# Two softmax attentions on one core: the matmuls of a step as tiles of 64 rows by 32 columns

## The chip, the cores and the metric

The kernel runs on one core of a Trainium2 chip. The core has five engines that run side by side, each with its own order of instructions: TensorE multiplies matrices (PE in the profile, PEld for its loading of weights), VectorE (DVE) and ScalarE (ACT) work element by element and can read the results of TensorE, GpSimd (POOL) works element by element on the large on-chip memory (SBUF) alone, and SyncE (SP) issues most of the transfers (DMA). TensorE writes its results to PSUM, a memory of eight banks, each of 128 partitions by 512 numbers of four bytes. A matmul multiplies a matrix of weights, loaded before, with data that stream through the array, one column after the other. The array of 128 rows by 128 columns can be used as several smaller tiles, and the profile shows several of them at work at the same time.

The metric is the device time of one execution in microseconds (us).

## What is computed

Two attentions over the same 2048 positions of 576 features are mixed by a gate. B has 32 heads with one shared key and value (unit 0 to 31 in the kernel), A has 32 heads with keys and values of their own (units 32 to 63). Each head is 18 wide.

```python
qkv = (x @ wqkv).reshape(B, S, 3, H, Dh)          # A; H = 32, Dh = 18
scores = einsum("bhqd,bhkd->bhqk", q, k) * Dh ** -0.5
p = softmax(scores, axis=-1)
o = einsum("bhqk,bhkd->bhqd", p, v)
a = o.transpose(0, 2, 1, 3).reshape(B, S, D) @ wo
# b is the same with q = x @ wq per head, one k = x @ wk and one v = x @ wv for all heads
g = sigmoid((x * gate_w).sum(-1, keepdims=True))
return g * a + (1 - g) * b                        # S = 2048, D = 576, f32
```

## The kernel before

**Stages.** First `project` (L205) and `project_v` (L249) compute queries, keys and values from x and the weights, as three products of a high and a low part, on the whole array. Then come 1024 steps, 16 for each of the 64 units. Step i of unit u works on keys 128 i to 128 i + 127 for scores and on queries 128 i to 128 i + 127 for maxima. The projection of the output (`out_proj`, L545) is cut into pieces, called units of work in the schedule, which are put between the steps; a tail adds the last head (`last_out`, L602).

**What a step does.** Queries and keys are split in two halves of 16 bits, so a product is one matmul over 54 rows (three products of 18 rows each), to which 2 rows with the maximum are added for the scores. The same rows lie twice in SBUF, from partition 0 (`SB`) and from partition 64 (`MB`).

- `step_scores` (L440; matmul L446): 128 keys by 512 queries, over partitions 0 to 55, into a bank of the pool `ps_s` (three banks). ScalarE takes the exponential of it (L453) into a tile `pt` in SBUF. Four of these make a step.
- `step_max` (L397; matmul L409): 128 queries by 512 keys, over partitions 64 to 117, into a bank of the pool `ps_m` (four banks). VectorE reduces it to a maximum per query (L418). These run 22 steps ahead (`LEAD`), since the maxima go into the scores. Every second step, one of its four maxima is replaced by the product `x` with the difference of two blocks of keys; ScalarE takes its Relu (L412), and a fused VectorE instruction (L415) adds it to another block and takes the maximum. So a pair of steps has eight score matmuls, eight of maxima (one of them `x`), nine instructions on ScalarE and seven on VectorE.
- `step_pv` (L455; matmul L459): the product of values (19 columns, one of them ones, for the sum) with `pt`, over 128 keys, in f32, for each of the four blocks of 512 queries. Block j goes to partitions 32 j to 32 j + 18 of one accumulator `acc` (one bank), so the four matmuls use four tiles of 128 rows by 32 columns. It adds up over the 16 steps.
- After step 15, `head_out` (L467) copies `acc` to SBUF on VectorE (L469), and SP's queue carries the parts to the rows of the head and to `sum_d`. The first value product of the next unit waits for the copy.

**Order.** The order of work on TensorE, and with it that on ScalarE and VectorE, is written out by hand. The loop at L695 goes through pairs of steps (T, T + 1) and through the words of a string: `sA0` is score block 0 of the first step of the pair, `mB2` maximum block 2 of the second step (of the unit 22 steps later), `x` the difference product, `p` and `f` the first and second half (256 columns each) of the value product of step T - 2, `P` both halves in one; `h` and `H` the two halves for step T - 1, `Q` both in one; `U` a unit of the output's projection, 12 matmuls over the whole array that take a bank of `ps_m`. `PLAIN` is the usual string, `UNIT` that of a pair with units, `END` that of a pair with T a multiple of 16, after which a head is copied out, `AFTER` that of the pair behind it, `ALONE` that of the last 11 pairs, when no maxima are left. `LEADS` and `FIRST` belong to the pairs before and at T = 0.

## Time and profile before

| | us |
|---|---|
| median of two runs | 2734.95 (2734.13 to 2735.77) |
| the profiled execution, its own time | 2735.79 |
| its span in the trace | 2734.0 |

The granted clock of TensorE was 0.991 of full speed in the mean. The first score of the steps starts at about 315 us and the last at about 2701 us of the span.

A page of the profile has the busy time of each engine, the span in slices, the DMA queues, the chain of work that ended last (followed back from the last instruction, at each step to what released it), and groups of instructions by line: `L453 ACT ACTIVATE pt<-ps ... x4052 | 2093.1, 637` says that line 453 ran 4052 times on ScalarE, was busy for 2093.1 us in all and 637 ns in the mean for one. Instructions of one engine overlap, so the mean of one is longer than its share of the time. The start-to-start distance in rows of the timeline (start in us, duration in us, engine, line, operation, output from input, count) is the better measure of what one costs. Some records of matmuls are missing from the trace, a few per cent.

### The profile page before, as it was taken

The numbers are of one execution on the slowest core, as the hardware profiler recorded it, in microseconds if no ns is written. First come the engines' busy times: TensorE is split into PE (matmuls) and PEld (weight loads), VectorE is DVE, ScalarE is ACT, GpSimd is POOL, SyncE is SP. The second block draws the span as 40 slices with busy tenths as digits, with TensorE's granted clock in tenths as the row PEclk, the third lists the DMA queues.
The fourth block names the chain that finished last, engine by engine and source line by source line (L and its number), as shares of the span: only waits on it lengthen the run. The fifth ranks groups of instructions, "written<-read, shape, count | busy, mean of one in ns | idle before, by whom it ended". The sixth has DMA issues, their size and how long they took to land.

```text
span 2734.0 us, 57725 instructions
## 1 busy us (share of the span) xinstructions
PE 2663.3 (97%) x22160; PEld 958.8 (35%) x22160; DVE 2430.7 (89%) x4582; ACT 2384.1 (87%) x4768; POOL 231.0 (8%) x438
## 2 busy tenths in 40 slices
PE   5899999999999999999999999999999999999999
PEld 3688522222222222222222333333333332223444
DVE  5345899999999999999999999999999999998875
ACT  3232499999999999999999999999999999998875
POOL 2221000001000200110110001000100020001000
PEclk9899999999999999999999999999999999999998
DMA  7232100001100100110132112112221122122312
GB/s 197 76 118 90 51 20 20 20 18 53 35 17 23 54 27 20 45 43 20 30 66 85 40 51 84 54 40 57 72 66 47 44 61 64 39 64 88 89 36 94
DMA packets 135321, 151.49 MB, mean 55 GB/s; under 512 B 55709, under 2 KB 104765, under 8 KB 133846
## 3 DMA queue, kind: packets, MB, share of 16 engines
q1 hardware_dynamic: 116156, 123.59, 16.2%
q10 hardware_dynamic: 14120, 13.65, 1.5%
q0 software_dynamic: 4768, 10.56, 1.2%
q8 instruction: 174, 2.85, 0.5%
q14 instruction: 103, 0.84, 0.1%
HBM read 92.02 MB, written 46.45 MB: 51 GB/s over the span
## 4 chain that ended last, share of the span: by engine, by line
ACT 54%; PE 37%; DVE 6%; DMA 2%; SPq 1%; issue 1%; DVEq 0%; ACTq 0%
ACT pt L453 48%; PE acc L459 12%; PE ps L446 11%; ACT xb L412 6%; PE ps L210 6%; PE pm L575 4%; DVE mx L418 3%; PE ps L252 2%; PE pm L409 2%; SPq L56 1%; DVE oe L469 1%; DVE junk L415 1%; DMA xs<-xT 0%; DVE oacc L629 0%; DVE oacc L583 0%
## 5 line engine op out<-in xcount | busy, mean ns | idle before, releaser
L453 ACT ACTIVATE pt<-ps 128x512 f32<-128x512 f32 x4052 | 2093.1, 637 | 68.4 <-PE pm L409 60.2
L418 DVE TENSOR_REDUCE mx<-pm 128x1 f32<-128x512 f32 x3096 | 1940.2, 682 | 89.5 <-PE pm L409 74.6
L446 PE MATMUL ps<-qs,ksb 56*128 56x512 f16 x2688 | 818.4, 380 | 10.8
L409 PE MATMUL pm<-ksb,qs 54*128 54x512 f16 x2364 | 738.5, 383 | 2.6 <-DVE mx L418 1.6
L459 PE MATMUL acc<-pt,vb 128*19 128x512 f32 (+1 forms) x6136 | 592.3, 458 | 1.9
L459 PE MATMUL acc<-pt,vg 128*19 128x256 f32 (+1 forms) x5664 | 579.5, 481 | 2.3 <-DVE oe L469 0.5
L409 PEld LDWEIGHTS <-qs 54*128 54x128 f16 x4096 | 330.0, 93 | 248.1 <-issue 195.2
L446 PE MATMUL ps<-qs,ksa 56*128 56x512 f16 x1364 | 404.4, 379 | 4.8 <-ACT pt L453 1.3
L446 PEld LDWEIGHTS <-ksb 56*128 56x128 f16 x2688 | 175.0, 94 | 622.5 <-issue 573.9
L409 PE MATMUL pm<-ksa,qs 54*128 54x512 f16 x1232 | 384.8, 382 | 0.6 <-ACT xb L412 0.4
L415 DVE CUSTOM_DVE_ANT_0 junk<-pm,xb 128x512 bf16<-128x512 f32 x500 | 339.9, 680 | 0.0
L412 ACT ACTIVATE xb<-pm 128x512 f32<-128x512 f32 x500 | 316.5, 633 | 0.0
L446 PEld LDWEIGHTS <-ksa 56*128 56x128 f16 x1408 | 89.3, 94 | 328.9 <-issue 299.0
L459 PEld LDWEIGHTS acc<-pt,vb 128*19 128x19 f32 x6136 | 104.1, 96 | 223.7 <-issue 206.6
L459 PEld LDWEIGHTS acc<-pt,vg 128*19 128x19 f32 x5664 | 96.0, 97 | 222.9 <-issue 204.9
L428 POOL TENSOR_SCALAR mt<-mt 128x32 f32<-128x32 f32 x64 | 18.6, 290 | 1616.4 <-DVE mt L426 1616.4
L214 ACT ACTIVATE ph<-ps,tv 128x512 f16<-128x512 f32 x56 | 38.5, 687 | 122.0 <-PE ps L210 114.5
L409 PE MATMUL pm<-kdb,qs 54*128 54x512 f16 x372 | 141.5, 380 | 0.0
L220 DVE SCALAR_TENSOR_TENSOR pl<-ps,tv,ph 128x512 f16<-128x512 f32 x56 | 42.0, 751 | 93.8 <-ACT ph L214 75.4
L210 PE MATMUL ps<-xh,wh 128*128 128x512 f32 x280 | 76.4, 403 | 3.3 <-DVE xh L277 2.6
L210 PE MATMUL ps<-xh,wl 128*128 128x512 f32 x280 | 75.1, 399 | 0.0
L469 DVE COPY oe<-acc 128x512 f32<-128x512 f32 x63 | 43.6, 692 | 30.0 <-PE acc L459 29.4
(123 smaller groups left out, 1253.8 us busy)
## 6 DMA issues: line engine op xcount, KB each, us to landing
qs<-qkh SPq DMA_DIRECT2D x244, 72.0 KB
qs<-qkl SPq DMA_DIRECT2D x122, 72.0 KB
onh<-oh SPq DMA_DIRECT2D x32, 256.0 KB
onl<-ol SPq DMA_DIRECT2D x32, 256.0 KB
oih<-onh SPq DMA_DIRECT2D x16, 512.0 KB
oil<-onl SPq DMA_DIRECT2D x16, 512.0 KB
ot<-oe SPq DMA_DIRECT2D x220, 36.0 KB
R<-r_d SPq DMA_DIRECT2D x55, 144.0 KB
```

The source lines that it names most:

```text
L210: nc.tensor.matmul(fp, w[a][:kr, k, :], X[b][:kr, k, cs], start=(n == 0), stop=(n == len(PROJ) - 1))
L220: nc.vector.scalar_tensor_tensor(l, fp, t, h, op0=OP.mult, op1=OP.subtract)
L252: nc.tensor.matmul(fp[:, 0:288], X[b][:kr, k, st_ * P:(st_ + 1) * P], w[a][:kr, k, :], start=(n == 0), stop=(n == len(PROJ) - 1))
L409: nc.tensor.matmul(pm, qs[u % 3][b:b + 54, i * P:(i + 1) * P], k, start=True, stop=True)
L412: nc.scalar.activation(MX["x", u, i], pm, AF.Relu)
L415: nc.vector.tensor_tensor_reduce(junk, pm, MX.pop(("x", u, i)), 1.0, -3e38, op0=OP.add, op1=OP.max, accum_out=MX[u][:, i, c:c + 1])
L418: nc.vector.tensor_reduce(MX[u][:, i, c:c + 1], pm, axis=AX.X, op=OP.max)
L446: nc.tensor.matmul(ps, kst(u)[b:b + 56, i * P:(i + 1) * P], qs[u % 3][b:b + 56, c * 512:(c + 1) * 512], start=True, stop=True)
L453: nc.scalar.activation(pt, ps, AF.Exp, scale=SCALE / LIFT ** 2)
L459: nc.tensor.matmul(acc[32 * j:32 * j + 19, a:b], v_of(u, i), PT[u, i, j][:, a:b], start=(i == 0 and a == 0), stop=(i == 15), skip_group_ch ...
L469: nc.vector.tensor_copy(oe, acc)
L575: nc.tensor.matmul(fp[:, 0:288], o[b][:r, t, s2 * P:(s2 + 1) * P], w[a][:r, t, 288 * hf:288 * hf + 288], start=(n == 0), stop=(n == 3 * nt ...
```

## The change

All matmuls of the steps use tiles of 64 rows by 32 columns. Scores and maxima are issued in quarters of 32 weight columns each; the value product is issued in two halves of 64 keys each, each half into an accumulator of its own, so that four times two matmuls stand in place of four. The second accumulator takes a bank from the pool for maxima, which keeps three. After a head, VectorE copies the first accumulator, ScalarE the second, and GpSimd adds the two; in the tail VectorE adds them. In the strings the value product comes in halves of 256 columns throughout; `END`, `P` and `Q` are gone, so that heads are copied out at the end of a pair, and the pair behind that (`AFTER`) starts its value products late. `UNIT` has the half `h` directly ahead of `U`.

```diff
-    ps_m = ctx.enter_context(tc.tile_pool(name="ps_m", bufs=4, space=PSUM))
+    ps_m = ctx.enter_context(tc.tile_pool(name="ps_m", bufs=3, space=PSUM))
...
-    acc = ps_o.tile([P, 512], F32, name="acc")
+    acc = [ps_o.tile([P, 512], F32, name=f"acc{h}") for h in range(2)]
...
+    def quarters(o, w, x):
+        for j in range(0, P, 32):
+            nc.tensor.matmul(o[j:j + 32, :], w[:, j:j + 32], x, start=True, stop=True, skip_group_check=True)
...
-        nc.tensor.matmul(pm, qs[u % 3][b:b + 54, i * P:(i + 1) * P], k, start=True, stop=True)
+        quarters(pm, qs[u % 3][b:b + 54, i * P:(i + 1) * P], k)
...
-        nc.tensor.matmul(ps, kst(u)[b:b + 56, i * P:(i + 1) * P],
-                         qs[u % 3][b:b + 56, c * 512:(c + 1) * 512], start=True, stop=True)
+        quarters(ps, kst(u)[b:b + 56, i * P:(i + 1) * P], qs[u % 3][b:b + 56, c * 512:(c + 1) * 512])
...
-        for j in range(4):
-            nc.tensor.matmul(acc[32 * j:32 * j + 19, a:b], v_of(u, i), PT[u, i, j][:, a:b],
-                             start=(i == 0 and a == 0), stop=(i == 15), skip_group_check=True)
+        for h in range(2):
+            r = slice(64 * h, 64 * h + 64)
+            for j in range(4):
+                nc.tensor.matmul(acc[h][32 * j:32 * j + 19, a:b], v_of(u, i)[r], PT[u, i, j][r, a:b],
+                                 start=(i == 0 and a == 0), stop=(i == 15), skip_group_check=True)
...
-        oe = L["work"].tile([P, 512], F32, name="oe", bufs=1)
-        nc.vector.tensor_copy(oe, acc)
+        oe, oe1 = (L["work"].tile([P, 512], F32, name=x, bufs=1) for x in ("oe", "oe1"))
+        nc.vector.tensor_copy(oe, acc[0])
+        nc.scalar.activation(oe1, acc[1], AF.Copy)
+        nc.gpsimd.tensor_tensor(oe, oe, oe1, op=OP.add)
...
-        nc.scalar.activation(oe, acc, AF.Copy)
+        nc.scalar.activation(oe, acc[1], AF.Copy)
+        nc.vector.tensor_tensor(oe, acc[0], oe, op=OP.add)
...
-    PLAIN = "sA0 mA2 sA1 mA0 sA2 mA3 P sA3 mB0 sB0 mB1 sB1 mB2 h sB2 mB3 sB3 x H"
-    UNIT = "sA0 mA2 sA1 mA0 sA2 mA3 P sA3 mB0 sB0 mB1 sB1 mB2 U sB2 mB3 sB3 x Q"
-    END = "sA0 mA2 sA1 mA3 sA2 mB0 P sA3 mB1 sB0 mA0 sB1 x Q sB2 mB2 sB3 mB3"
-    AFTER = "sA0 mA2 p sA1 mA0 sA2 mA3 sA3 x f sB0 mB0 sB1 mB1 h sB2 mB2 sB3 mB3 H"
-    ALONE = "sA0 sA1 P U sA2 sA3 U sB0 sB1 h U sB2 sB3 H U"
+    PLAIN = "sA0 mA2 sA1 mA0 p sA2 mA3 sA3 mB0 f sB0 mB1 sB1 mB2 h sB2 mB3 sB3 x H"
+    UNIT = "sA0 mA2 sA1 mA0 p sA2 mA3 sA3 mB0 f sB0 mB1 sB1 mB2 h U sB2 mB3 sB3 x H"
+    AFTER = "sA0 mA2 sA1 mA0 sA2 mA3 sA3 mB0 sB0 mB1 p sB1 mB2 f sB2 mB3 h sB3 x H"
+    ALONE = "sA0 sA1 p f U sA2 sA3 U sB0 sB1 h U sB2 sB3 H U"
...
         order = LEADS if T < 0 else FIRST if T == 0 else ALONE if alone else UNIT if units else \
-            END if T % 16 == 0 else AFTER if order is END else PLAIN
+            AFTER if T % 16 == 2 else PLAIN
```

More of the change, by code (lines that the diff above doesn't have):

```diff
@@ L85, in gated_mix_kernel @@
     ones_r = dram.tile([2, S], F16, name="ones_r")
-    acc = ps_o.tile([P, 512], F32, name="acc")
-    nc.vector.memset(acc, 0.0)
+    acc = [ps_o.tile([P, 512], F32, name=f"acc{h}") for h in range(2)]
+    for h in range(2):
+        nc.vector.memset(acc[h], 0.0)
+    def quarters(o, w, x):
+        for j in range(0, P, 32):
+            nc.tensor.matmul(o[j:j + 32, :], w[:, j:j + 32], x, start=True, stop=True, skip_group_check=True)
     nc.vector.memset(vb, 1.0)
@@ L456, in step_pv @@
     def step_pv(u, i, a, b):
-        for j in range(4):
-            nc.tensor.matmul(acc[32 * j:32 * j + 19, a:b], v_of(u, i), PT[u, i, j][:, a:b],
-                             start=(i == 0 and a == 0), stop=(i == 15), skip_group_check=True)
+        for h in range(2):
+            r = slice(64 * h, 64 * h + 64)
+            for j in range(4):
+                nc.tensor.matmul(acc[h][32 * j:32 * j + 19, a:b], v_of(u, i)[r], PT[u, i, j][r, a:b],
+                                 start=(i == 0 and a == 0), stop=(i == 15), skip_group_check=True)
         if b == 512:
```

## The prediction

> **What bounds the kernel now.** I read the page first (busy shares, then the chain of waits), then the windows by stage, then the copies of the accumulator, which come once per head and give the period, and last the order of time on TensorE, ScalarE and VectorE around one pair of steps.
>
> ```profile
> PE 2663.3 (97%) x22160; PEld 958.8 (35%) x22160; DVE 2430.7 (89%) x4582; ACT 2384.1 (87%) x4768; POOL 231.0 (8%) x438
> ...
> ACT 54%; PE 37%; DVE 6%; DMA 2%; SPq 1%; issue 1%; DVEq 0%; ACTq 0%
> ```
>
> The chain is more than half ScalarE and more than a third TensorE. A chain that changes hands like this says that neither is the only bound, so I look at the stages.
>
> ```profile
> 320.00:1320.00 1000.00, 989.84 (x8877) 278.70 (x8874) 979.51 (x1866) 985.59 (x1999) 59.77 (x123) 1.00 0.10 29
> 2460.00:2650.00 190.00, 189.63 (x1473) 77.64 (x1466) 162.77 (x313) 157.54 (x308) 15.23 (x24) 1.00 0.26 77
> ```
> ```profile
> L469 DVE COPY oe<-acc x5: 691/691/692, 359.0 to 502.5; 128x512 f32<-128x512 f32 x5
> L469 DVE COPY oe<-acc x4: 691/692/692, 1892.4 to 2006.2; 128x512 f32<-128x512 f32 x4
> L469 DVE COPY oe<-acc x4: 691/692/692, 2536.6 to 2672.4; 128x512 f32<-128x512 f32 x4
> ```
>
> The columns of the first two rows are the busy times of PE, PEld, DVE, ACT and POOL, the granted clock, and DMA. From 320 to 1320 us all three big engines are at 98 to 99%; at the end (2460 to 2650) only PE is full, ACT is at 83% and DVE at 86%. The copies give the period of a head (8 pairs of steps): (502.5-359.0)/4 = 35.88 us without units of the output projection, (2006.2-1892.4)/3 = 37.9 with them, (2672.4-2536.6)/3 = 45.3 at the end. 35.88/8 = 4.485 us per pair. What would each engine need alone?
>
> ```profile
> 1012.40 0.68 DVE L415 CUSTOM_DVE_ANT_0 junk<-pm,xb 128x512 bf16<-128x512 f32 x1
> 1013.01 3.67 DVE L418 TENSOR_REDUCE mx<-pm 128x1 f32<-128x512 f32 x6
> 1016.60 0.68 DVE L415 CUSTOM_DVE_ANT_0 junk<-pm,xb 128x512 bf16<-128x512 f32 x1
> ...
> 1013.44 2.56 ACT L453 ACTIVATE pt<-ps 128x512 f32<-128x512 f32 x5 [0.32 <-PE pm L409]
> 1015.85 0.64 ACT L412 ACTIVATE xb<-pm 128x512 f32<-128x512 f32 x1
> 1016.33 4.08 ACT L453 ACTIVATE pt<-ps 128x512 f32<-128x512 f32 x8
> ```
>
> DVE undisturbed: one fused maximum (1012.40 to 1013.01, 0.61) and six reductions (1013.01 to 1016.60, 0.598 each) make 4.20 us per pair. ACT: five exponentials from 1013.44 to 1015.85 are 0.48 each, the Relu 0.48; eight exponentials and one Relu are 9 x 0.478 = 4.30. PE:
>
> ```profile
> 1000.27 0.63 PE L459 MATMUL acc<-pt,vb 128*19 128x256 f32 x8
> 1000.83 0.39 PE L446 MATMUL ps<-qs,ksb 56*128 56x512 f16 x1
> ...
> 1001.93 0.39 PE L446 MATMUL ps<-qs,ksb 56*128 56x512 f16 x1
> 1001.93 0.39 PE L409 MATMUL pm<-ksb,qs 54*128 54x512 f16 x1
> 1002.15 0.38 PE L446 MATMUL ps<-qs,ksb 56*128 56x512 f16 x1
> ...
> 1002.41 0.39 PE L409 MATMUL pm<-ksb,qs 54*128 54x512 f16 x1
> 1002.72 1.06 PE L459 MATMUL acc<-pt,vb 128*19 128x512 f32 x8
> 1002.72 0.14 PEld L459 LDWEIGHTS acc<-pt,vb 128*19 128x19 f32 x8 [0.23 <-issue]
> 1003.71 0.39 PE L446 MATMUL ps<-qs,ksb 56*128 56x512 f16 x1
> ```
>
> A score (L446, rows 0 to 63) and a maximum (L409, rows 64 to 127) start together at 1001.93, and the next pair comes 0.22 later. A block of the value product lasts 0.99 for 512 columns (1002.72 to 1003.71) and 0.56 for 256 (1000.27 to 1000.83): 256 columns are worth 0.43, and 0.13 is left over at the way out. On the way in, 1002.41 to 1002.72 is 0.31 where 0.22 would do: 0.09. Each block thus costs 0.22 us of changing over. A plain pair now has eight score-and-maximum slots (1.76), 1024 columns of values (1.72) and three blocks (0.66): 4.14. So PE 4.14, DVE 4.20 and ACT 4.30, coupled by three and four PSUM banks, make 4.485.
>
> **The change, part by part.** *Quarters and halves.* If the 0.22 hangs on the change of tile shape, it goes. Four tiles side by side cost little: the eight weight loads of one block lie within 0.14 us, each about 0.096 long. A score and a maximum become eight matmuls on eight tiles, a value block eight on the same eight tiles per pass; each stream is as long as before. I allow 0.03 us more per block for the longer file. PE per pair: 1.76 + 1.72 + 4 x 0.03 = 3.60, 0.54 less. The columns of the array are not better filled by it; only the changing over is saved.
>
> The switches around a unit of the projection stay, since L575 still uses the whole array:
>
> ```profile
> 2599.67 1.05 PE L459 MATMUL acc<-pt,vg 128*19 128x512 f32 x8
> ...
> 2602.84 0.38 PE L409 MATMUL pm<-ksa,qs 54*128 54x512 f16 x1
> 2603.15 0.80 PE L575 MATMUL pm<-woh,oih 128*128 128x288 f32 x4
> ...
> 2604.94 0.39 PE L446 MATMUL ps<-qs,ksb 56*128 56x512 f16 x1
> ...
> 2605.47 1.05 PE L459 MATMUL acc<-pt,vg 128*19 128x512 f32 x8
> ```
>
> A pair with a unit has two blocks of 512 columns and takes 5.80 here (2599.67 to 2605.47). A unit keeps PE from 2603.15 to 2604.94, 1.79, plus 0.09 on the way in: 1.88. 1.76 + 1.72 + 2 x 0.22 + 1.88 is 5.80: at the end PE alone sets the time, and the count of PE holds.
>
> The Trainium skill, "TensorEngine Tiling (Array Packing)", Key Properties, says that a change of tiling mode, not of tile, drains TensorE. By that rule all 0.66 us per plain pair of the blocks go, which is the sum just made; the rows' 0.09 and 0.13 agree with it.
>
> *Instructions.* This is what the change pays.
>
> ```profile
> L409 PEld LDWEIGHTS <-qs 54*128 54x128 f16 x4096 | 330.0, 93 | 248.1 <-issue 195.2
> L446 PEld LDWEIGHTS <-ksb 56*128 56x128 f16 x2688 | 175.0, 94 | 622.5 <-issue 573.9
> L446 PEld LDWEIGHTS <-ksa 56*128 56x128 f16 x1408 | 89.3, 94 | 328.9 <-issue 299.0
> L459 PEld LDWEIGHTS acc<-pt,vb 128*19 128x19 f32 x6136 | 104.1, 96 | 223.7 <-issue 206.6
> ...
> q8 instruction: 174, 2.85, 0.5%
> ```
>
> 4096 maxima and 4096 scores in 512 pairs are 16 matmuls per pair; each value matmul is recorded as two (two passes), so three blocks give 24. With as many weight loads that is 80 instructions per pair; afterwards it is 64 + 64 matmuls and as many loads, 256. Queue q8 (packets, MB, share of 16 engines) fetched 2.85 MB of instructions for 22160 matmuls and loads; 3.2 times as many in the steps make about 8.6 MB, still under 2% of the DMA engines. A weight load lasts 93 to 96 ns whether it has 128 columns or 19, so quarters of 32 columns should last as long and hide under the streams. What the trace does not show is PE taking 256 instructions in 4.3 us, 17 ns each. Its ends: nothing, by the eight loads within 0.14 us (under 10 ns from start to start), and by the mean of the whole stage, 8877 matmuls and as many loads in 1000 us, 56 ns each, which would be a pair of 14.4 us (an end that is too far out, since PE had nothing more to take there). I take nothing, since the burst is the row nearest to what will run, and keep a slower feed as a rival.
>
> *Head output.* Per head ACT gets a copy of the second accumulator, like L412 0.48; DVE's copy stays; POOL gets a sum of 128x512.
>
> ```profile
> L522 POOL TENSOR_TENSOR ot<-ot,R 128x512 f32<-128x512 f32 x32 | 40.9, 1279 | 117.8 <-DMA qs<-qkh 40.9 <-DMA kda<-kdh 26.9 <-DMA vg<-v_d 23.2
> ...
> L424 DVE TENSOR_REDUCE m<-mx 128x16 f32<-128x64 f32 x64 | 14.1, 220 | 2.2
> L426 DVE STREAM_TRANSPOSE mt<-m 128x32 f32<-128x32 f32 x64 | 13.6, 212 | 6.6
> ```
>
> POOL's sum is 1.28 us by L522, and POOL is 8% busy. The copies out to the head's rows, queued on SP, wait for it, and with them the loads behind them on SP; those are for heads that are two to three periods away, so I cost it at nothing. If that cover were gone it would be 1.3 us per head, 80 us in all. ACT's copy waits for the last value block; behind it on ACT stand the next pair's exponentials, and the new head's first value product waits for both copies. After a head the first product now comes after ten slots of scores and maxima, at least 2.2 us later, so this too is hidden. Floors per head: ACT 72 x 0.478 + 0.48 = 34.9; DVE 8 x 4.20 + 0.69 + 0.22 + 0.21 = 34.7; PE 28.8.
>
> *Three banks for maxima.* DVE can lag by 1.8 us instead of 2.4. In a pair without a unit PE is away from maxima for one block at a time (0.46), which three banks cover. Around a unit they don't: from the last maximum, 0.22, the half block that now stands before it, 0.46, and the unit, 1.88, make 2.56 us to the next. One of the three banks belongs to the unit, so DVE has at most two reductions (1.2) when it begins at 0.68, is dry at 1.9, and gets the unit's result at about 2.55: 0.65 idle, plus about 0.2 until the next maximum. With 0.46 for the addition to the output a unit costs DVE some 1.3 us. Today it costs (37.9-35.88)/1.5 = 1.35 per unit. Nothing is won there; nothing is lost either.
>
> *The sum.* Units run in some 25 of the 64 heads, 21 with 1.5 on average and four at the end with one in nearly each pair. Without units: ACT's 34.9 and 0.2 for the coupling, 35.1 against 35.88, 0.78 x 38 = 30 us. With 1.5 units: DVE 34.7 + 1.5 x 1.3 + 0.3 = 36.9 against 37.9, 1.0 x 21 = 21. At the end: PE 8 x (3.60+1.88) = 43.8, DVE 8 x (4.20+1.3) + 1.1 = 45.1, with some coupling 45.5, against 8 x 5.80 = 46.4: 0.9 x 4 = 4. The last steps, where scores run without maxima and PE is the bound, I put at 5, from 0.44 us per pair over the 11 pairs; the projections before and the tail at nothing. Together 60 us off the profiled run, whose span is 2734.0 and whose time is 2735.8, 0.8 over the median of 2734.95: 2675.
>
> **The rivals.** (1) *The gain is eaten by coupling.* ACT stays at 98.6%, gets 0.48 per head more, and DVE with three banks stops PE more often. Per head 35.6 in place of 35.1 gives 0.3 x 38 = 11, and nothing in the unit heads: 2715. For it: ACT and DVE floors lie within 0.2 us of each other, so each stall of one reaches the other; against it: PE now has 0.7 us per pair to make up for stalls.
>
> (2) *Slower: the gap hangs on the change of number format (f16 to f32 and back) and not on the tile shape.* Then four blocks cost 4 x 0.22 = 0.88 in place of 0.66, PE has 3.48 + 0.88 + 0.12 = 4.48 per pair, over ACT's 4.30. Plus what it now loses by coupling, 0.2, that is 4.68 or 0.2 x 512 = 102 more: 2840. It decides as soon as PE's pair is over 4.30. The tail speaks against it:
>
> ```profile
> 2707.59 0.29 PE L575 MATMUL pm<-wol,endh 110*128 110x288 f32 x1
> 2707.73 0.60 PE L616 MATMUL pm<-ident,oe 128*128 128x128 f32 x4
> ```
>
> Projection and transposes have different formats and the same shape, and follow at 0.14, no later than projections among themselves.
>
> (3) *Slower: TensorE cannot take the instructions.* From 4.485/256 = 17.5 ns each on, the pair gets longer; at 20 ns it is 5.12, 0.63 x 512 = 325 more: 3060. The same time comes about if the two halves of the value product run one after the other (1.72 more per pair, 5.3). For it: no stretch of this trace is that dense. Against it: the burst of loads.
>
> The Trainium skill, "TensorE: Matmul & The Clock Gate", Part 1, states that matmuls start at least about 25 ns apart however small they are. Read over all tiles, an estimate by that page is 128 x 25 ns = 3.2 us per pair, under the bound; counted for loads too it would be 6.4. No run here shows the sustained rate.
>
> (4) *Faster still.* The stalls around units shrink too, because PE refills all banks at once: 0.6 less per unit, 64 units, 38 more: 2637.
>
> **How the numbers follow.** Forecast 0.52, (1) 0.16, (2) 0.13, (3) 0.13, (4) 0.06. The forecast's own spread, from a coupling of 0 to 0.6 us per head and 1.0 to 1.6 per unit, is 2650 to 2700. Two per cent, about what a measurement can tell from no change, is 55 us: the line is at 2680, so some 0.32 of the 0.52 lies beyond it. Faster 0.32 + 0.06 = 0.38; within 0.20 + 0.16 = 0.36; slower 0.26. The range runs from 2640, which leaves (4) out, to 2850, which takes (2) in and leaves (3) out: 0.19 outside.
>
> **What would show it.** Each step right: a value block of 256 columns 0.45 to 0.47 from its first start to the next score; a score 0.22 after the maximum before it even where a block lies next to it; 35.1 us between copies of the accumulator; ACT at 99% and PE clearly idle. Wrong: 0.09 and 0.13 still there (2); quarters starting 20 ns apart or idle time of PE put down to issue (3); DVE waiting for PE's maxima between units (1). The projection's units should still cost 1.3 us.

## The result, and the profile after

| | before | after |
|---|---|---|
| median of two runs, us | 2734.95 | 2845.06 (2840.32 to 2849.79) |
| ratio, 95% interval | | 1.0403 (1.0327 to 1.0478) |
| the profiled execution, its own time, us | 2735.79 | 2849.79 |
| its span, us | 2734.0 | 2847.9 |

The kernel became 4% slower. Two of the experiments below (`half_4banks`, `half_3banks`) had executions at a mean granted clock of 0.71 to 0.74, some 600 us longer; their times and ratios are those of their other executions.

The page of the changed kernel answers first: busy time by engine, then the queue of instructions, then the chain of waits by engine, then one group of instructions.

```profile
PE 2668.4 (94%) x67704; PEld 1541.9 (54%) x67704; DVE 2449.4 (86%) x4584; ACT 2405.8 (84%) x4831; POOL 311.0 (11%) x501
...
q8 instruction: 530, 8.68, 1.3%
...
PE 56%; ACT 17%; DVE 16%; issue 8%; DMA 2%; SPq 1%; ACTq 0%; POOLq 0%; POOL 0%; DVEq 0%
...
L479 POOL TENSOR_TENSOR oe<-oe,oe 128x512 f32<-128x512 f32 x63 | 80.3, 1274 | 1036.4 <-ACT oe L478 530.8
```

No engine does much more than it did: ACT has 21.7 us more (63 copies), DVE 18.7, PE 5. The time went into waits. In the chain ACT's share fell from 54% to 17%, PE's rose from 37% to 56% and DVE's from 6% to 16%, and 8% are issue. The windows by stage (busy time of PE, PEld, DVE, ACT, POOL in the stretch) and the copies of the first accumulator (first and last start) say the same by stage:

```profile
345.00:1320.00 975.00, 927.94 (x27016) 503.65 (x27015) 935.38 (x1769) 947.09 (x1925) 91.33 (x143) 1.00 0.11 31
2560.00:2760.00 200.00, 196.01 (x4588) 120.72 (x4579) 160.97 (x305) 150.23 (x301) 19.25 (x29) 1.00 0.24 69
```
```profile
L477 DVE COPY oe<-acc x5: 681/683/692, 381.2 to 527.7; 128x512 f32<-128x512 f32 x5
L477 DVE COPY oe<-acc x4: 691/692/693, 1886.1 to 2003.4; 128x512 f32<-128x512 f32 x4
L477 DVE COPY oe<-acc x5: 691/692/693, 2582.0 to 2775.9; 128x512 f32<-128x512 f32 x5
```

In the plain stage all three engines were at 98 to 99% before; now PE is at 95%, DVE at 96% and ACT at 97%. A plain head takes (527.7-381.2)/4 = 36.6 us, against 35.88 before and 35.1 in the forecast; one with units (2003.4-1886.1)/3 = 39.1, against 37.9 and 36.9; one at the end (2775.9-2582.0)/4 = 48.5, against 45.3 (over the last three heads; over four, as here, it is 45.6) and 45.5. The first copy comes at 381.2 instead of 359.0, so 22 us are lost before the first head is done.

And yet the part of the change that the forecast was most in doubt about does what it should. The timeline (start, duration, engine, line, operation, count) of TensorE around a half of the value product:

```profile
862.14 0.40 PE L95 MATMUL ps<-qs,ksb 56*32 56x512 f16 x4
862.16 0.40 PE L95 MATMUL pm<-ksb,qs 54*32 54x512 f16 x4
...
862.36 0.63 PE L467 MATMUL acc<-pt,vb 64*19 64x256 f32 x16
...
862.79 0.40 PE L95 MATMUL ps<-qs,ksb 56*32 56x512 f16 x4
862.82 0.39 PE L95 MATMUL pm<-ksb,qs 54*32 54x512 f16 x4
```

From the slot to the values 0.22, from the values to the next slot 0.43: the 0.09 on the way in and the 0.13 on the way out are gone to the last hundredth, although f16 and f32 still alternate. TensorE got its time back; the question is who took it.

### The profile page after: what moved, and what is told of

Read it like the earlier page. It is cut to its first block, busy times and chain, and to the rows that moved or that the text cites. A ratio compares the mean times of both kernels' runs of the same rounds, so it can differ in the third digit from the quotient of the medians.

```text
span 2847.9 us, 153612 instructions
## 1 busy us (share of the span) xinstructions
PE 2668.4 (94%) x67704; PEld 1541.9 (54%) x67704; DVE 2449.4 (86%) x4584; ACT 2405.8 (84%) x4831; POOL 311.0 (11%) x501
## 4 chain that ended last, share of the span: by engine, by line
PE 56%; ACT 17%; DVE 16%; issue 8%; DMA 2%; SPq 1%; ACTq 0%; POOLq 0%; POOL 0%; DVEq 0%
PE ps L95 19%; PE acc L467 18%; ACT pt L459 13%; DVE mx L425 12%; PE ps L217 6%; PE pm L95 6%; PE pm L585 4%; ACT xb L419 3%; DVE junk L422 3%; PE ps L259 2%; SPq L56 1%; ACT oe L478 1%; DMA xs<-xT 0%; DVE oacc L640 0%; DVE wabs L169 0%
## 5 line engine op out<-in xcount | busy, mean ns | idle before, releaser
L95 PE MATMUL ps<-qs,ksb 56*32 56x512 f16 x10752 | 998.6, 381 | 54.9 <-ACT pt L459 23.3
L95 PE MATMUL pm<-ksb,qs 54*32 54x512 f16 x9456 | 896.6, 382 | 25.1 <-DVE mx L425 13.8
L95 PEld LDWEIGHTS <-qs 54*32 54x32 f16 x16384 | 549.5, 89 | 340.1 <-issue 254.8
L467 PE MATMUL acc<-pt,vb 64*19 64x256 f32 x16384 | 718.0, 377 | 4.3 <-issue 4.3
L467 PE MATMUL acc<-pt,vg 64*19 64x256 f32 x16384 | 712.5, 378 | 5.1 <-issue 2.7
L95 PEld LDWEIGHTS <-ksb 56*32 56x32 f16 x10752 | 430.1, 90 | 460.7 <-issue 363.8
L95 PE MATMUL ps<-qs,ksa 56*32 56x512 f16 x5456 | 498.7, 381 | 25.9 <-ACT pt L459 10.5
L95 PE MATMUL pm<-ksa,qs 54*32 54x512 f16 x4928 | 469.9, 382 | 5.9 <-DVE mx L425 0.5
L467 PEld LDWEIGHTS acc<-pt,vg 64*19 64x19 f32 x16384 | 290.7, 95 | 70.5 <-issue 6.8
L467 PEld LDWEIGHTS acc<-pt,vb 64*19 64x19 f32 x16384 | 293.1, 95 | 53.8 <-issue 6.1
```

The source lines that it names most:

```text
L95: nc.tensor.matmul(o[j:j + 32, :], w[:, j:j + 32], x, start=True, stop=True, skip_group_check=True)
L467: nc.tensor.matmul(acc[h][32 * j:32 * j + 19, a:b], v_of(u, i)[r], PT[u, i, j][r, a:b], start=(i == 0 and a == 0), stop=(i == 15), skip_gr ...
```

## The experiments

Times are medians in us; ratios are to the kernel before, measured in the same session (2733 to 2735), with a 95% interval. Edits are against the changed kernel where nothing else is said.

| kernel | tiles of a step | order | banks for maxima | time | ratio (95%) |
|---|---|---|---|---|---|
| before | 64/128 rows | old | 4 | 2734.95 | 1 |
| `before_3banks` | 64/128 rows | old | 3 | 2930.80 | 1.0725 (1.0709 to 1.0741) |
| `strings_4banks` | 64/128 rows | new | 4 | 2832.71 | 1.0359 (1.0344 to 1.0375) |
| `strings_3banks` | 64/128 rows | new | 3 | 2878.98 | 1.0528 (1.0512 to 1.0544) |
| `tiles_old_strings` | 64 x 32 | old | 3 | 2839.98 | 1.0385 (1.0369 to 1.04) |
| after | 64 x 32 | new | 3 | 2845.06 | 1.0403 (1.0327 to 1.0478) |
| `strings_4banks_early` | 64/128 rows | new, values early | 4 | 2776.09 | 1.0147 (1.013 to 1.0164) |
| `after_early` | 64 x 32 | new, values early | 3 | 2800.88 | 1.0251 (1.0233 to 1.0268) |

### The lost bank

The kernel before with one bank less and nothing else changed:

```diff
-    ps_m = ctx.enter_context(tc.tile_pool(name="ps_m", bufs=4, space=PSUM))
+    ps_m = ctx.enter_context(tc.tile_pool(name="ps_m", bufs=3, space=PSUM))
```

> The kernel before with three banks for maxima in place of four, nothing else (one bank stays empty). Theory A (the lost bank costs the lead 20 us and a unit some 0.3 us, the rest of the loss has other causes): 2734 + 20 + 64 x 0.3 = about 2775, heads without units nearly unchanged (36.0). Theory B (the lost bank is the whole loss): 2845, heads without units 36.5 or more.

Measured: 2930.80, 196 us more than before and far beyond what any theory expected. The window of its plain stage, and rows of its timeline:

```profile
345.00:1320.00 975.00, 968.28 (x8114) 217.96 (x8115) 910.91 (x1701) 918.69 (x1826) 57.51 (x114) 1.00 0.10 28
```
```profile
1000.95 2.56 ACT L453 ACTIVATE pt<-ps 128x512 f32<-128x512 f32 x5 [0.42 <-PE pm L409]
...
1003.36 0.64 ACT L412 ACTIVATE xb<-pm 128x512 f32<-128x512 f32 x1
...
1003.63 0.38 PE L446 MATMUL ps<-qs,ksb 56*128 56x512 f16 x1
1004.05 0.37 PE L409 MATMUL pm<-ksb,qs 54*128 54x512 f16 x1
...
1003.65 0.69 DVE L418 TENSOR_REDUCE mx<-pm 128x1 f32<-128x512 f32 x1 [0.18 <-PE pm L409]
```

ACT and DVE are at 93 to 94% and wait for PE. PE in turn waits for a bank for its maxima: the one at 1004.05 starts 0.42 after the score before it, as soon as the Relu on ACT, which ends at 1003.36 + 0.64 = 1004.00, has read its bank. A score's record is 0.38 long and hides most of this wait, so PE looks 99% busy. By the trace, 581 maxima in this window start 0.04 us after an instruction on DVE releases their bank, and 178 after a Relu on ACT does; in the kernel before it is 209 and none. The fourth bank was what let the three run side by side.

In the changed kernel the lost bank acts in the lead as well, where maxima are computed between the value projections. There the bank pool of the scores is idle, so it can lend one:

```diff
-        pm = ps_m.tile([P, 512], F32, name="pm")
+        pm = ps_s.tile([P, 512], F32, name="ps") if low and c == 3 else ps_m.tile([P, 512], F32, name="pm")
```

> The changed kernel, but in the pairs before T = 0 the fourth maximum of each step goes to a bank of the scores' pool, so that four banks take part again there. Theory A (the time before the steps grew because the fourth maximum waits for the first one's reduction, three banks being one too few): the first score comes some 20 us earlier, at about 317 to 319 us, and the whole takes 2825. Theory B (the lead got slower because changing between the projection's whole array and the small tiles costs more): no change, 2845, first score at 338.

Measured: 2822.92, ratio 1.0323 (1.0307 to 1.0338). The windows of the stage for the changed kernel and for `lead4`, the rows of PE in each, and the copies of `lead4`:

```profile
260.00:310.00 50.00, 43.62 (x412) 33.93 (x411) 27.63 (x46) 7.33 (x19) 0.31 (x1) 1.00 0.19 62
```
```profile
293.19 0.61 PE L95 MATMUL pm<-ksb,qs 54*32 54x512 f16 x12
294.38 0.40 PE L95 MATMUL pm<-ksb,qs 54*32 54x512 f16 x4 [0.58 <-DVE mx L425]
```
```profile
260.00:310.00 50.00, 50.00 (x524) 41.86 (x523) 35.75 (x61) 8.65 (x21) 1.07 (x4) 1.00 0.24 81
```
```profile
294.10 0.61 PE L95 MATMUL pm<-ksb,qs 54*32 54x512 f16 x12
294.34 0.39 PE L95 MATMUL ps<-ksb,qs 54*32 54x512 f16 x4
```

```profile
L477 DVE COPY oe<-acc x5: 678/679/692, 358.0 to 504.6; 128x512 f32<-128x512 f32 x5
```

Four maxima are issued in a row there. Three go, the fourth waits 0.58 us for a reduction, and PE, the bound of this stage, is idle 13% of it. With the fourth in the other pool PE is full, the first copy comes at 358.0 (last row) instead of 381.2, and 22 us are back.

Whether the bank could be taken from the scores instead (on top of `after_early`, below):

```diff
-    ps_s = ctx.enter_context(tc.tile_pool(name="ps_s", bufs=3, space=PSUM))
-    ps_m = ctx.enter_context(tc.tile_pool(name="ps_m", bufs=3, space=PSUM))
+    ps_s = ctx.enter_context(tc.tile_pool(name="ps_s", bufs=2, space=PSUM))
+    ps_m = ctx.enter_context(tc.tile_pool(name="ps_m", bufs=4, space=PSUM))
```

> after_early with two banks for scores and four for maxima in place of three and three. Theory A (the maxima's banks are the scarce ones): the lead is 22 us shorter as in lead4, a unit costs 1.35 instead of 1.8, together 2755. Theory B (ScalarE needs its third bank just as much): heads without units over 36.5, slower than 2801.

Measured: 3043.55, ratio 1.1131 (1.111 to 1.1152), 243 us over `after_early`. The maxima have their fourth bank back in it, so the scores' third bank is dearer still. No pool has a bank to spare.

### The order

The kernel before with the strings of the change (and its rule for when heads are copied out), first with four banks, then with three:

```diff
-            END if T % 16 == 0 else AFTER if order is END else PLAIN
+            AFTER if T % 16 == 2 else PLAIN
```

> The kernel before with the changed kernel's strings and its own four banks, tiles and accumulator. Theory A (the strings cost TensorE 0.22 us per pair for the fourth block, but spread the blocks better; with four banks the spread is worth little): heads of 35.9 to 36.5, 2740 to 2770. Theory B (the strings are better at any number of banks, by the 52 us that they gave at three): 2685.

> The kernel before with three banks for maxima and with the changed kernel's strings (value products in four blocks of 256 columns per pair), tiles and accumulator as before: it differs from the changed kernel in the tile shapes and the second accumulator alone. Theory A (each block costs 0.22 us of changing over, and it is on the path): a pair has one more of them than in the kernel before with three banks, 8 x 0.22 = 1.8 us more per head, heads of 40.2 instead of 38.43, about 3020; the tiles are then worth some 175 us at equal banks and strings. Theory B (the strings are the better ones at three banks, and the tiles give little): 2850 or less.

Measured: 2832.71 and 2878.98. On the old tiles the new order costs 98 us by itself, more than expected. Three banks cost 46 on top of it, which lies between what the theories expected. In the new order the bank is cheaper than in the old (46 against 196): in the same window of `strings_3banks` only 26 maxima start on the release of the Relu's bank, where `before_3banks` has 178.

One place of that can be read in the trace of the changed kernel, in the pair after a head (`AFTER`); the rows of ACT:

```profile
860.34 0.78 ACT L478 ACTIVATE oe<-acc 128x512 f32<-128x512 f32 x1
860.81 2.26 ACT L459 ACTIVATE pt<-ps 128x512 f32<-128x512 f32 x4
863.77 2.07 ACT L459 ACTIVATE pt<-ps 128x512 f32<-128x512 f32 x4 [0.69 <-PE acc L467]
```

The pool of `pt` has 12 tiles. Eight hold the two steps whose values are not yet multiplied; four exponentials fill the rest; the fifth waits until the two halves of the value product, put off behind the tenth and the twelfth score or maximum of the pair, give a tile back. So in `AFTER` the values go four words of the string earlier:

```diff
-    AFTER = "sA0 mA2 sA1 mA0 sA2 mA3 sA3 mB0 sB0 mB1 p sB1 mB2 f sB2 mB3 h sB3 x H"
+    AFTER = "sA0 mA2 sA1 mA0 sA2 mA3 p sA3 mB0 f sB0 mB1 sB1 mB2 h sB2 mB3 sB3 x H"
```

> The changed kernel with the value products of AFTER two to three slots earlier (p ahead of sA3, f ahead of sB0). Theory A (once per head ScalarE's fifth exponential of the pair waits for one of the 12 tiles for exponentials, all of which are held until the late value product has read them): the gap of 1.04 us per head goes, some 57 heads, 55 to 60 us less, 2785 to 2790, heads of 35.5 us instead of 36.57. Theory B (the gap comes from the copies of the two accumulators): TensorE waits at p for ScalarE's copy instead, no gain or slower.

> As strings_4banks, with AFTER's value products two to three slots earlier as in after_early. Theory A (twelve tiles for exponentials hold up ScalarE once per head here too): 0.8 us less per head than strings_4banks, about 45 us less. Theory B (that wait belongs to the second accumulator's copy): no difference.

Measured: on the small tiles 2800.88, 44 less than after; on the old tiles 2776.09, 57 less than `strings_4banks`. The copies of `after_early`, those of `strings_4banks_early`, and the window of the latter's plain stage:

```profile
L477 DVE COPY oe<-acc x5: 678/678/692, 380.7 to 524.0; 128x512 f32<-128x512 f32 x5
```
```profile
L469 DVE COPY oe<-acc x5: 681/681/681, 361.0 to 505.5; 128x512 f32<-128x512 f32 x5
```
```profile
320.00:1320.00 1000.00, 998.89 (x10581) 260.94 (x10581) 971.07 (x1854) 996.81 (x1987) 59.38 (x122) 1.00 0.10 28
```

A plain head falls from 36.6 to (524.0-380.7)/4 = 35.8, 0.8 in each. On the old tiles it is (505.5-361.0)/4 = 36.1, and PE's records fill the stage: the strings have four value blocks in a pair where the old ones had three, and each block pays 0.22 there. That, by this count, is the part of the new order that only the new tiles pay back.

The other side, the new tiles with the old strings:

```diff
-            AFTER if T % 16 == 2 else PLAIN
+            END if T % 16 == 0 else AFTER if order is END else PLAIN
```

> The changed kernel with the strings of the kernel before (P, Q and END, blocks of 512 columns), three banks and small tiles. Theory A (three banks cannot cover a block of 512 columns, 0.87 us and the slot ahead of it, whatever the tiles: this is why the kernel before with three banks lost 197 us): slower than the changed kernel, heads of 37 to 38, 2870 to 2900; the shorter blocks of the new strings are needed because of the lost bank. Theory B (the new strings are the loss, since with four banks they cost 99 us): about 2845 - 99 = 2746, and the old order is the better one with the small tiles too.

Measured: 2839.98, neither theory's number but the same as after within the spread of after's two runs. With small tiles the old strings are no better than the new.

### The second accumulator

`after_early` without ACT's copy of the second accumulator and without the sum on POOL; the second half of the keys is missing from the output.

```diff
-        nc.scalar.activation(oe1, acc[1], AF.Copy)
-        nc.gpsimd.tensor_tensor(oe, oe, oe1, op=OP.add)
```

> after_early, but a head is taken from the first accumulator alone: ScalarE's copy of the second and GpSimd's sum are left out, so half of the keys is missing from the result of all heads but the last. Theory A (ScalarE sets the heads of 35.77 us): 0.48 x 63 = 30 us less, 2770. Theory B (the heads are set by how the three banks couple the engines): 10 us less at most.

Measured: 2761.64, ratio 1.0099 (1.0084 to 1.0114), 39 less than `after_early`. That is 39/63 = 0.62 us per head, where ACT's copy takes 0.47 from its start to that of the next instruction (860.34 to 860.81 above).

### The units of the projection

With three banks a unit should cost DVE 1.3 us, as before, and it costs more; by the copies of the head with units above, 39.1 - 36.6 = 2.5 for 1.5 units, 1.7 each. Three tries at the reason. First, the half of the value product that stands ahead of the unit goes behind it:

```diff
-    UNIT = "sA0 mA2 sA1 mA0 p sA2 mA3 sA3 mB0 f sB0 mB1 sB1 mB2 h U sB2 mB3 sB3 x H"
+    UNIT = "sA0 mA2 sA1 mA0 p sA2 mA3 sA3 mB0 f sB0 mB1 sB1 mB2 U sB2 mB3 h sB3 x H"
```

> The changed kernel with U ahead of h in UNIT, as it stood in the kernel before. Theory A (ScalarE and VectorE run dry behind a unit because half a value block was put ahead of it): 0.44 us less per unit, 64 units, 28 us less, 2817, and the idle time of ScalarE behind a unit falls from 1.84 to about 1.4. Theory B (VectorE is dry because one of only three banks is taken by the unit, whatever stands ahead): no more than 5 us less.

Measured: 2842.37, ratio 1.0399 (1.0383 to 1.0414), 3 us less than after: no more than its spread. Then `lead4` and `after_early` together, with the unit's result in a bank of the scores:

```diff
-                    fp = ps_m.tile([P, 512], F32, name="pm")
+                    fp = ps_s.tile([P, 512], F32, name="ps")
```

> The changed kernel with the edits of lead4 and after_early, and the projection's unit in a bank of the scores' pool in place of one of the maxima's. Theory A (a unit costs 1.75 us and not 1.35 because it takes one of the three banks for maxima): 1.4 per unit, 64 x 0.35 = 22 us under 2779, that is 2757. Theory B (ScalarE runs dry just as VectorE does, so a bank is missed in either pool): 2779 or slower.

Measured: 2783.11, ratio 1.0174 (1.0159 to 1.0189); the two single edits add up to 2845 - 22 - 44 = 2779 without it. Then the three good edits together (`combined`: `lead4`, `unit_first`, `after_early`), and on top of that the unit split in two halves of six matmuls, in a bank of the scores:

```diff
-    UNIT = "sA0 mA2 sA1 mA0 p sA2 mA3 sA3 mB0 f sB0 mB1 sB1 mB2 U sB2 mB3 h sB3 x H"
+    UNIT = "sA0 mA2 sA1 mA0 p sA2 mA3 sA3 mB0 f sB0 mB1 U sB1 mB2 h sB2 mB3 U sB3 x H"
```

> The changed kernel with the three edits lead4, after_early and unit_first at once. Theory A (they mend different places): 2845 - 22 - 44 - 3 = 2776. Theory B (they mend the same wait): over 2790. Either way slower than the kernel before, since units keep costing 1.7 us each.

> combined, with each unit of the projection in two halves of six matmuls at two places of the pair (after mB1 and after mB3), its result in a bank of the scores' pool. Theory A (a unit costs 1.75 us because TensorE stays away from scores and maxima for 2.5 us at a time, more than three banks hold): 0.6 us less per unit, 64 units, 40 us less than 2778, about 2738. Theory B (the two more changes of shape and the bank held from one half to the other cost as much): 2778 or slower.

Measured: `combined` 2777.96, ratio 1.016 (1.0145 to 1.0176); split 2781.36, ratio 1.0171 (1.0154 to 1.0188). Neither moving the unit's bank to the other pool, nor moving the half ahead of it, nor splitting its stay on PE makes it cheaper by more than some 0.15 us a unit; the split also holds its bank for longer, so it does not clear the length of the stay. The rows of one unit in the changed kernel:

```profile
2641.42 0.63 PE L467 MATMUL acc<-pt,vg 64*19 64x256 f32 x16
2641.98 0.79 PE L585 MATMUL pm<-woh,oih 128*128 128x288 f32 x4
...
2643.75 0.40 PE L95 MATMUL ps<-qs,ksa 56*32 56x512 f16 x4
...
2643.86 0.46 DVE L593 TENSOR_TENSOR oacc<-pm,oacc 128x288 f32<-128x288 f32 x1 [1.04 <-PE pm L585]
...
2644.26 1.09 ACT L459 ACTIVATE pt<-ps 128x512 f32<-128x512 f32 x2 [1.63 <-PE pm L95]
...
2645.12 0.69 DVE L425 TENSOR_REDUCE mx<-pm 128x1 f32<-128x512 f32 x1 [0.17 <-PE pm L95]
```

DVE is idle 1.04 before the addition and 0.17 after the next reduction, 1.2 in all, where 0.85 was forecast; ACT, which the forecast did not count here, is idle 1.63 at the same time. How much of this hangs on the number of banks the next section shows.

### What TensorE's gain is worth, with the costs taken away

The order of `combined`, with only the first 64 keys of each step in the value product and one accumulator, so that a fourth bank is free; half of the keys is missing from the output. Small tiles, no second copy, and half of the value matmuls. Then the same with three banks:

```diff
-        for h in range(2):
+        for h in range(1):
```

> The strings of combined with small tiles, but the value product over the first 64 keys of each step alone: the second accumulator, its copy and GpSimd's sum are left out, so half of the keys is missing from the result; the bank that comes free goes to the maxima, which have four. TensorE's time is nearly that of both halves, since these run side by side. Theory A (the small tiles save TensorE what was forecast, and the lost bank and the second copy take it back): faster than the kernel before by 60 us or more, 2675 or less, heads of 34.5 to 35.2 and units at 1.4. Theory B (the small tiles themselves bring nothing): 2734 or more.

> As half_4banks, with three banks for maxima (one stays empty). Theory A (the lost bank weighs as much with small tiles as the 46 us between strings_4banks and strings_3banks, or more): 2675 + 46 = 2720 or more, 22 of it in the lead. Theory B (with small tiles TensorE is fast enough to do with three): within 25 us of half_4banks, all of it in the lead.

Measured: four banks 2724 (ratio 0.9964, 0.9945 to 0.9983), three banks 2763 (1.0109, 1.009 to 1.0129). With everything in favour of the small tiles, only 9 us are gained on before (2733 in the same session), much less than expected. The window and the copies of `half_4banks`, then those of `combined`:

```profile
320.00:1320.00 1000.00, 918.98 (x21732) 471.20 (x21735) 990.85 (x1900) 998.44 (x2037) 60.89 (x125) 1.00 0.11 31
```
```profile
L477 DVE COPY oe<-acc x5: 679/681/683, 358.7 to 499.8; 128x512 f32<-128x512 f32 x5
```
```profile
320.00:1320.00 1000.00, 972.91 (x28325) 528.04 (x28328) 981.79 (x1860) 992.16 (x2021) 94.10 (x150) 1.00 0.11 31
```
```profile
L477 DVE COPY oe<-acc x5: 678/679/692, 359.6 to 502.9; 128x512 f32<-128x512 f32 x5
```

A plain head of `half_4banks` takes (499.8-358.7)/4 = 35.3. ACT is busy 99.8% of the time with 2037 instructions, 998.44/2037 = 0.490 each. That is not what one instruction needs, though: the records of ACT overlap, so a wait of up to some 0.28 us leaves no idle time. Its rows of one pair tell more:

```profile
1002.57 0.77 ACT L419 ACTIVATE xb<-pm 128x512 f32<-128x512 f32 x1
1003.04 4.21 ACT L459 ACTIVATE pt<-ps 128x512 f32<-128x512 f32 x8
1006.98 0.76 ACT L419 ACTIVATE xb<-pm 128x512 f32<-128x512 f32 x1
```

From the Relu to the next start are 0.47, but the eight exponentials take 3.94, 0.49 each. Taken one by one, 1149 of the 2035 distances from start to start in this window are 0.477. Nearly once in each pair, 217 times, the distance is 0.55, and this exponential begins 0.02 after the end of a score on PE: ACT waits for PE. Most of the others are 0.49, for a reason that the trace does not show. In the other direction PE waits 188 times for ACT to empty a bank of the scores, 77 us in all. So 72 instructions at 0.478 would be 34.4, and a head is 0.9 longer even here. In `combined`, with the copy, (502.9-359.6)/4 = 35.8 is 0.9 over 73 x 0.478 = 34.9. From 35.88 before, a plain head thus falls to 35.3 in the most favourable kernel run here, and the second copy takes 0.5 of that 0.6 back.

The total also hides a part of the gain: between the first and the last copy `half_4banks` takes 2285.4 against 2313.4 before, 28 less, but behind the last copy 78.5 against 61.6, much of it at a granted clock of 0.50 (2660 to 2680 us of its span).

The bank is worth 2763.5 - 2723.8 = 40 us on small tiles, and the copies show where. The profiled execution of `half_3banks` had its full granted clock from 2009 us of its span on; here are its copies without units from there, its copies with units, three in two heads, and those of `half_4banks` for the same heads with units:

```profile
L477 DVE COPY oe<-acc x5: 679/683/693, 2861.2 to 3002.2; 128x512 f32<-128x512 f32 x5
```
```profile
L477 DVE COPY oe<-acc x5: 691/691/693, 2328.2 to 2480.2; 128x512 f32<-128x512 f32 x5
L477 DVE COPY oe<-acc x5: 691/691/692, 1719.4 to 1869.4; 128x512 f32<-128x512 f32 x5
```

A plain head takes (3002.2-2861.2)/4 = 35.3 with three banks, as with four. One with units takes (2480.2-2328.2)/4 = 38.0 with three and (1869.4-1719.4)/4 = 37.5 with four, so a unit costs 2.7/1.5 = 1.8 with three and 2.2/1.5 = 1.5 with four. From the 32nd copy to the last, through the heads with units and those at the end, it is 1208.6 against 1189.9, 19 us; with the 22 of the lead that is all of it. `no_second_copy`, with three banks and both halves of the values, agrees: 35.3 and 38.1.

### The feed of instructions

The chain has 8% issue, 226 us in 1748 pieces. Of these, 210 us lie in pieces of at most 0.4 us between one instruction of the chain and the next; only six pieces, 11.7 us in all, are longer than 1 us. They are stalls like these two of PE, during which ACT and DVE run dry too:

```profile
674.15 0.44 PE L467 MATMUL acc<-pt,vb 64*19 64x256 f32 x8 [1.74 <-issue]
...
932.52 0.39 PE L95 MATMUL ps<-qs,ksb 56*32 56x512 f16 x3 [1.86 <-issue]
```

In the changed kernel five of PE's stalls are longer than 1 us, 250 to 279 us apart, and each begins 7 to 10 us after the first of a row tile's 144 KB loads of `R` is issued; all of PE's stalls on issue in the steps are some 11 us. The kernels with old tiles whose traces were read for this (`before`, the three `strings` kernels and `before_3banks`) have none of more than 0.5 us on PE. If these loads delay the packets of instructions, spreading them over three pairs should help (edit on top of `combined`, for six of the eight row tiles):

```diff
+            if not at_end and t not in (3, 7) and (u - u0) % 3 == 2:
+                yield
```

> combined, with the eight loads of reciprocals (R) of a row tile spread over three pairs of steps in place of one, for six of the eight row tiles. Theory A (TensorE's stalls of about 2 us, which end 1.2 to 1.8 us after a packet of instructions, come from these loads, which hold up the packet): fewer and shorter stalls, 5 to 9 us less than 2778. Theory B (they come from the rate of instructions alone): as many stalls, 2778.

Measured: 2777.04, ratio 1.0162 (1.0147 to 1.0176), against 2777.96. PE's stalls of more than 0.3 us fell from eight (9.4 us) to four (7.3 us), and the time did not change; 2 us are less than the runs differ among themselves. That the loads and the instructions meet is so far only argued from their times, and the stalls seen account for some 11 us, not for 110.

## Why the prediction was wrong

**The sum and what came.** The forecast has the first copy at 359.0, 2258.4 between the first and the last copy (2313.4 less 30, 21 and 4), and 56.6 behind it, a span of 2674. Measured were 381.2, 2775.9 - 381.2 = 2394.7, and 72.0. So 22 are lost ahead of the first copy, 136 between the copies and 15 behind: 174 in all. Of the 136, plain heads have (36.6-35.1) x 38 = 57, heads with units (39.1-36.9) x 21 = 46, those at the end (48.5-45.5) x 4 = 12; the rest, 21, holds the stalls on issue, some 11. By cause, as the paragraphs below have it, three terms of nearly the same size failed: the late value product (44), the coupling (some 41, an estimate from the heads) and the lost bank (40, as measured between two kernels without the second accumulator). The 15 behind the last copy and the 11 of the stalls come on top; some 20 stay open.

**Right: TensorE's own part.** It said that "the changing over is saved", and it is: 0.22 and 0.43 around a block, as quoted. The Trainium skill, "TensorEngine Tiling (Array Packing)", Key Properties, says that a change of mode drains TensorE and a change of tile does not; the trace agrees, 0.09 and 0.13 with the change of mode, nothing without. Rival (2), the change of number format, gave the time that came, 2840, for a reason that the rows refute. That the two halves run one after the other, the other form of rival (3), is refuted too: sixteen matmuls of 64x256 lie within 0.63. And "256 instructions in 4.3 us" cost nothing but the stalls above. POOL's sum was 1.27, as forecast (1.28).

**Wrong: "so this too is hidden" (the first value product after ten slots).** The copies are hidden: they have ended by 861.12, and the product begins at 862.36. The forecast asked what waits for the copies, and not what the late product holds: eight of 12 `pt` tiles. That is 44 us on the small tiles, 0.8 in each head, shown by `after_early`, and 57 on the old. The ten words of the string are also five scores and five maxima, which is 1.1 us at the forecast's own 0.22 a slot and not 2.2.

**Wrong in size: "0.2 for the coupling".** The forecast took 9 x 0.478 per pair for ACT, 34.9 a head with the second copy, and only 0.2 on top. The 0.478 holds for most instructions, but with the late product mended a plain head is 35.8, 0.9 over this sum, and in `half_4banks` it is 0.9 over it too. By the starts there, ACT waits for PE's scores nearly once in each pair, and PE for the banks that ACT empties. That is 0.7 x 59 = 41 us in the heads without and with units, and all of "0.78 x 38 = 30" went with it: below 35.88 there was 0.1. Rival (1) named the right place, coupling, and priced it at 0.5 a head; it is 0.7, but not for the reason given there, the three banks, which cost a plain head nothing. The copy was put at 0.48 a head, 30 us in all; taken away it gives 39.

**Wrong: "Nothing is won there; nothing is lost either" (three banks).** For a plain head of the new tiles the forecast's count holds: 35.3 with three banks and with four. It fails in the lead, which the forecast put "at nothing" and where the bank has 22 us (`lead4`), and around the units and at the end, where it has 19 more; together 40 on small tiles. A unit was put at 1.3 and costs 1.7 to 1.8, of which the bank makes 0.3. The forecast counted how long DVE can lag, and left out ACT, which is idle 1.63 behind a unit where DVE is idle 1.2. What makes a unit 1.5 and not 1.35 with four banks stays open. `strings_4banks_early` has 1.8 with four banks too ((39.7-36.1)/2 by its copies), but there PE's records fill the stage, and `UNIT` has two blocks more than in the kernel before: 1.35 + 2 x 0.22 = 1.8.

On the old tiles the same bank costs 196 in the old order and 46 in the new. There the forecast's count misses ACT as well: the bank of `x` comes free only when the Relu has read it, and the maxima behind it wait (`before_3banks`). The Trainium skill's same page, Gotcha 1, says that different row tiles write to different banks and so press on PSUM; this case gives the price, 40 to 196 us for one of the seven banks that scores and maxima had. Under "PSUM Bottleneck" the page says that with a faster TensorE the emptying of PSUM may become the bound; `half_4banks` agrees, PE at 92% and ACT at 99.8%.

**Wrong: the end at 5 us of gain.** Behind the last copy it is 72.0 against 61.6. A timeline row of PE, the row of DVE that it goes back to, and a window some us later; the last row is DVE's in the kernel before:

```profile
2800.10 0.37 PE L585 MATMUL pm<-woh,endh 110*128 110x288 f32 x1 [2.27 <-DVE endh L130]
```
```profile
2798.80 0.69 DVE L525 TENSOR_TENSOR ot<-ot,R 110x512 f32<-110x512 f32 x1 [10.38 <-DMA R<-r_d]
```
```profile
2805.00:2809.00 4.00, 3.64 (x61) 1.41 (x46) 1.75 (x4) 2.23 (x4) 0.00 (x0) 0.50 0.02 4
```
```profile
2691.52 0.69 DVE L515 TENSOR_TENSOR ot<-ot,R 110x512 f32<-110x512 f32 x1 [10.38 <-DMA R<-r_d]
```

DVE waited 10.38 us for the load of `R` before the change too, 2691.52 - 2672.4 = 19.1 behind the last copy; now it is 2798.80 - 2775.9 = 22.9 behind it, PE stands still for 2.27 until `endh` comes, and a few us later its granted clock is 0.50 (1.00 from 2690 to 2710 us in the kernel before). By these rows the end hangs on that load and not on PE's pairs; no run was made on it.

**The whole, by two paths.** From before: one bank less, +196 (2931); small tiles with the second accumulator, -91 (2840); new strings, +5 (2845). Or: new strings, +98 (2833); one bank less, +46 (2879); small tiles, -34 (2845). The tiles do pay, 34 to 91 us, but only back what the bank and the order have taken. No kernel run here that computes everything beats the one before: `strings_4banks_early`, `combined_spread` and `combined` with 2776 to 2778 are next. `combined` shows that 67 of the 110 us were mendable, 22 in the lead, some 44 in `AFTER`; what is left is the copy, the units, the end, and the coupling that leaves a plain head at 35.8.

## What to carry to other kernels

When several engines are within a few per cent of each other, work saved on one of them is worth the distance to the time that the others reach together, and not to the sum of the next one's instructions: 35.3 here where the sum is 34.4. Busy time does not show this difference when records overlap; starts do. A buffer that a change takes away must be priced by an experiment or by the widest range, stage by stage and for every engine that holds it: its cost here was nothing in a plain head of the new tiles, 40 us in the rest of that kernel, and 196 in the old one. And of a step that is put later, ask not only who waits for its result but what it keeps occupied until it runs.

## What the runs showed of the hardware

Eight tiles of 64 x 32 start almost together: four quarters of a score and four of a maximum, 0.39 to 0.40 us long, begin within 0.04 us (862.79 to 862.83), and sixteen value matmuls fit into 0.63. By their starts in the trace these are two groups of eight, 0.22 apart, in each of which the starts lie 2 to 16 ns apart. The Trainium skill, "TensorE: Matmul & The Clock Gate", Part 1, has some 25 ns as the least distance; across tiles it is less here.

The clock fell in a stage without any idle time of PE. `half_3banks`, in which rows 64 to 127 have no value matmuls, ran in the profiled execution for more than 1000 us at 0.50 with PE never idle, and later at 0.99 in the same loop; the windows:

```profile
500.00:1500.00 1000.00, 1000.00 (x14072) 480.04 (x14064) 690.21 (x1229) 707.51 (x1318) 39.09 (x80) 0.50 0.07 20
2000.00:2500.00 500.00, 480.50 (x10320) 240.99 (x10317) 466.94 (x885) 476.20 (x966) 32.90 (x64) 0.99 0.21 59
```

In the windows of the steps shown above for the kernels that use both halves of the rows the clock was 1.00. Whether the empty rows are the cause, no run tells; no other kernel had it than `half_3banks` and `half_4banks`.
